# A written engine order for the last stage of a fused attention and expert kernel, and spare products beside the last four weight pieces

## The chip, the cores and the metric

The kernel runs on one core of a Trainium2 chip. Five engines work side by side, each through its own instructions in order: TensorE (PE, the matrix products; its weight loads are listed as PEld), VectorE (DVE), ScalarE (ACT), GpSimd (POOL) and SyncE (SP), whose queue issues the DMA transfers here. The metric is the device time of one execution in microseconds (us), as the median of several runs. A profile is one more execution with a recorder on.

## The reference

Three layers follow each other on 4608 tokens of width 512. Attention with pooled keys gives `x`; a soft mixture of 8 experts with 32 slots mixes it; a feed-forward layer with a softmax gate and a layer norm ends it.

```python
logits = x @ phi                                   # 4608 x 32
d = softmax(logits, over tokens); slot_input = d.T @ x
slot_out[e] = relu(slot_input[e] @ w1[e]) @ w2[e]  # 8 experts, 4 slots each
x = softmax(logits, over slots) @ slot_out

h = x @ w_in                                       # 4608 x 1024
solu = h * softmax(h)
ln = (solu - mean(solu)) / sqrt(var(solu) + 1e-6) * g_ln
out = ln @ w_out                                   # 4608 x 512
```

## The kernel before

The first half of the program computes attention, the logits and the slots. Then the expert weights stream in. The second expert layer takes `w2` in 16 pieces of 1 MB; `second(e, fh)` multiplies each piece as it lands (L856). After some pieces PE also runs a spare product, whose result nobody reads: `ident` times a part of the piece just used (L887). The dictionary `DUM` says after which pieces, and how many columns; before, after pieces 9, 10 and 11. The spare result shares its PSUM bank with `pcs`, the column sums of `w_out` that `out_sums` adds up (L848, L849). What comes after piece 15 is a chain: copies of the slot outputs (ACT L901), small products `ps` (PE L904), their copy `so` (DVE L908), the products `pM` of the slots with `w_in` (PE L924), and their copies (ACT L928), from which the first rows of `h` are computed. Part of `w_in` still has to be converted from doubles to floats beside that (ACT L745, L746; DVE L747, L748; POOL or DVE L749), and the last products `pM` wait for it.

The last stage goes over 36 tiles of 128 tokens. For tile `i` the steps are: `front_pe` (PE L1084: a pair of products makes `h`, in one of two pairs of PSUM banks), `front_max` (DVE L1089), `front_exp` (ACT L1096), `front_u` (DVE L1102, frees `h`), `front_mean` (POOL L1108), `front_square` (ACT L1113), `front_stats` (POOL, eight small instructions, L1119 to L1129; L1124 makes `sr`, L1126 makes `b`); then `turn_scale` (ACT L1138), `turn_high` (DVE L1151) and `turn_low` (DVE L1155), whose results two transposing DMAs turn (SP L1159 and L1162); then `products` (PE: 16 products with the high half `vhi`, L1174 and L1175, and 8 with the low half `vlo`, L1177, added up in one of two PSUM banks `o`); then `rows_out` (ACT L1187 copies `o` to `ob`, which frees the bank; every third tile a DMA writes the rows). The fronts run `LAG` = 4 tiles ahead of the products.

Up to a step called `E` each engine's order is written out in a list of step names, and kept. From there to the end, `mctx.close()` leaves the order to a scheduler, except for the last tile's products, which are cut in two halves of 256 columns (L1274 to L1279):

```python
    run("E")
    mctx.close()
    run("")
    for m in range(NPRO, NT):
        j = m + LAG
        if j < NT:
            front(j)
        if j - 1 < NT:
            turn(j - 1)
        if m < NT - 1 or not LS:
            products(m, 0, 8)
            rows_out(m)
```

Of the kernel before, what the change touches and what calls it, by code (L numbers as in the profile page):

```python
# [8 lines left out]
F32 = mybir.dt.float32  # L9
# [10 lines left out]
P = 128  # L20
# [3 lines left out]
NT = NP * NB * NR  # L24
# [5 lines left out]
DM = 512  # L30
DF = 1024
NE = 8
NFC = DF // P
# [15 lines left out]
LS = 2  # L49
# [36 lines left out]
def moe_attention_kernel(ctx: ExitStack, tc, q, k, v, phi, w1, w2, w_in, w_out, g, out):  # L86
# [151 lines left out]
    psE = None  # L238
    actx = ExitStack()
    if True:  # L240
# [166 lines left out]
        def turn(n, c):  # L407

            pt = st["pt", n, c] = psA.tile([P, NR, P], F32, tag="at", bufs=B.get("at",2), name=f"pt{n}{c}")
            for r in range(NR):  # L410
                pe.transpose(pt[:, r, :], a_buf[n % NA][:, r, CH[c]:CH[c] + P], ident)  # L411
# [282 lines left out]
    psE = ectx.enter_context(tc.tile_pool(name="psE", bufs=1, space=PSUM, reuse_waits="tile"))  # L694
# [31 lines left out]
    if True:  # L726
        ex = ctx.enter_context(tc.tile_pool(name="ex", bufs=1, side="left", reuse_waits="tile"))
        cvp = ctx.enter_context(tc.tile_pool(name="cvp", bufs=2, side="left", reuse_waits="tile"))
        mctx = ExitStack()
# [108 lines left out]

        p2 = psE.tile([P, DM], F32, name="p2")

        DUM = {9: (512,), 10: (512,), 11: (512,)}
        spare = psE.tile([P, DM], F32, name="spare")
        csum = T_all.rearrange("p g s -> p (g s)")

        def out_sums(c):
# [8 lines left out]
        def second(e, fh):  # L854
            for c in range(4):
                pe.matmul(p2[32 * c:32 * c + 32, :], hTm[:, 4 * fh + c, 32 * e:32 * e + 32], w2t[e, fh, c],  # L856
                          start=(e == 0 and fh == 0), stop=(e == NE - 1 and fh == 1), tile_position=(0, 32 * c))
# [8 lines left out]
        for x in range(2 * NE):  # L866
# [18 lines left out]
            second(x // 2, x % 2)  # L885
            for nn in DUM.get(x, ()):
                pe.matmul(spare[:, 0:nn], ident, w2t[x // 2, x % 2, 3][:, 0:nn], start=True, stop=True)  # L887
# [6 lines left out]
        def op(name, needs, f, *args):  # L894
            ops[name] = allops[name] = needs.split(), f, args
# [44 lines left out]
        for c in (6, 7):  # L940
# [9 lines left out]
                 'Gy6 R4 Fe9 Ga7 P5a Ff9 P5bl Gc7 Ff8 R5 Gx7 Fg8 Fg9 Ga8 Gb8 Gy7 Gx8 Gc8 Gy8 K1').split()  # L950
        assert sorted(set(steps)) == sorted(steps)
# [2 lines left out]
        def run(until):  # L954
            while steps:
                name = steps.pop(0)
                if name == until:
                    return done.add(name)
                needs, f, args = ops.pop(name)
                assert done.issuperset(needs), (name, needs)  # L960
                f(*args)
                done.add(name)
# [14 lines left out]
    LAG = 4  # L977
# [153 lines left out]
    def front(i):  # L1131
        for f in (front_pe, front_max, front_exp, front_u, front_mean, front_square, front_stats):
            f(i)
# [34 lines left out]
    def products(i, c0, c1, what="hl"):  # L1168
        hi, lo = hi_t[i], lo_t[i]
        if c0 == 0 and "h" in what:  # L1170
            po_t[i] = ps2.tile([P, DM], F32, tag="o", name=f"o{i}")
        po = po_t[i]
        for c in range(c0, c1) if "h" in what else ():
            pe.matmul(po, hi[:, c, :], W_hi[:, c, :], start=(c == 0), stop=False)  # L1174
            pe.matmul(po, hi[:, c, :], W_lo[:, c, :], start=False, stop=False)  # L1175
        for c in range(c0, c1) if "l" in what else ():
            pe.matmul(po, lo[:, c, :], W_hi[:, c, :], start=False, stop=(c == NFC - 1))  # L1177

    def rows_scaled(i):
        blk, r = divmod(i, NR)  # L1180
        if r == 0:
            o_t[blk] = wk2.tile([P, NR, DM], F32, name="ob")
        ob = o_t[blk][:, r, :]
        if i < NRAW:
            act.activation(ob, csum, AF.Copy, scale=rs_t[i][:, 0:1])
        else:
            act.activation(ob, po_t.pop(i), AF.Copy, scale=rs_t.pop(i))  # L1187

    def rows_sum(i):
        y, ob = rs_t.pop(i), o_t[i // NR][:, i % NR, :]  # L1190
        dve.scalar_tensor_tensor(ob, po_t.pop(i), y[:, 1:2], ob, ALU.mult, ALU.add)

    def rows_kept(i):
        blk, r = divmod(i, NR)
        if blk == NT // NR - 1:
            sp.dma_start(out[blk, :, DM * r:DM * r + DM], o_t[blk][:, r, :])
        elif r == NR - 1:
            sp.dma_start(out[blk], o_t.pop(blk).rearrange("p r d -> p (r d)"))

    def rows_out(i):  # L1200
        rows_scaled(i)
        if i < NRAW:
            rows_sum(i)
        rows_kept(i)
# [44 lines left out]
            op(f"R{i}", f"P{i}bl", rows_scaled, i)  # L1249
    op("K0", f"Q{NR - 1}", rows_kept, NR - 1)  # L1250
    op("K1", f"R{2 * NR - 1}", rows_kept, 2 * NR - 1)
    run("E")
    mctx.close()
    run("")
    assert not ops, ops.keys()
    for m in range(NPRO, NT):
        j = m + LAG
        if j < NT:
            front(j)
        if j - 1 < NT:  # L1260
            turn(j - 1)
        if m < NT - 1 or not LS:
            products(m, 0, 8)
            rows_out(m)

    if LS:

        hi, lo, r, ob = hi_t[NT - 1], lo_t[NT - 1], rs_t[NT - 1], o_t[NT // NR - 1][:, NR - 1, :]
        for x in range(LS):
            w = DM // LS  # L1270
            cols = slice(w * x, w * x + w)
            po = ps2.tile([P, DM], F32, tag="vT" if x % 2 else "o", name=f"o{NT - 1}{x}")[:, 0:w]
            for c in range(NFC):
                pe.matmul(po, hi[:, c, :], W_hi[:, c, cols], start=(c == 0), stop=False)  # L1274
                pe.matmul(po, hi[:, c, :], W_lo[:, c, cols], start=False, stop=False)  # L1275
            for c in range(NFC):
                pe.matmul(po, lo[:, c, :], W_hi[:, c, cols], start=False, stop=(c == NFC - 1))  # L1277
            act.activation(ob[:, cols], po, AF.Copy, scale=r)  # L1278
            sp.dma_start(out[NT // NR - 1, :, DM * (NR - 1):DM * NR][:, cols], ob[:, cols])  # L1279


# [39 lines left out]
```

## Time and profile before

| | |
|---|---|
| median of 3 runs | 449.43 us (447.93 to 451.49) |
| the profiled execution, own time | 448.71 us |
| its span in the trace | 446.9 us |
| PE busy in the span | 397.3 us (89%) |
| DVE, ACT, POOL busy | 314.6, 296.9, 236.8 us |
| matmul group L1174, idle before it | 5.1 us, of which 4.9 after ACT's `ob` |

The span is what the trace covers; the time adds 1.8 us around it. An engine's busy time adds up its instructions; for PE their ends are modelled and overlap, so that start-to-start distances say more than busy shares. Idle time in a row stands in brackets with the instruction that ended it.

### The profile page before, as it was taken

How to read it: one execution, taken by the hardware profiler on the slowest of the kernel's cores; microseconds unless marked ns; L12 is line 12 of the kernel's file. 1: busy time of each engine (PE TensorE's matmuls, PEld its weight loads, DVE VectorE, ACT ScalarE, POOL GpSimd, SP SyncE). 2: the span in 40 equal slices, each digit the busy share in tenths (PEclk: the TensorE clock that was granted, in tenths of full speed). 3: DMA queues.
4: the chain of work that ended last, by engine and by line, in shares of the span. 5: the costliest groups of instructions: out<-in, count | busy, mean ns of one | idle time of the engine just before them, and what ended most of it. 6: DMA issues, size and time to landing. Idle time of an engine off the chain costs nothing. (4 is left out here: it accounts for less than half of the span.)

```text
span 446.9 us, 8280 instructions
## 1 busy us (share of the span) xinstructions
PE 397.3 (89%) x2977; PEld 230.8 (52%) x2977; DVE 314.6 (70%) x513; ACT 296.9 (66%) x664; POOL 236.8 (53%) x427
## 2 busy tenths in 40 slices
PE   4689979987999797877979999999999999999897
PEld 4578868866977423321335544444444444444445
DVE  4897995799863634796489997667677776776730
ACT  3588976767795508763458987666667676666651
POOL 5588775568331046953105787656464464554620
PEclk9989996999899898989699999999999999999999
DMA  8999999673779798999000199565564763955853
GB/s 260 414 394 418 397 416 354 215 248 129 264 293 341 255 346 333 381 417 415 34 0 1 25 205 179 94 160 144 93 164 90 170 154 63 184 136 103 166 127 108
DMA packets 87801, 97.07 MB, mean 217 GB/s; under 512 B 70097, under 2 KB 74961, under 8 KB 82769
## 3 DMA queue, kind: packets, MB, share of 16 engines
q1 hardware_dynamic: 87760, 96.55, 68.6%
q8 instruction: 23, 0.38, 0.3%
q14 instruction: 18, 0.14, 0.1%
HBM read 70.32 MB, written 9.44 MB: 178 GB/s over the span
## 5 line engine op out<-in xcount | busy, mean ns | idle before, releaser
L1174 PE MATMUL o<-W_hi,vhi 128*128 128x512 f16 x280 | 106.2, 379 | 5.1 <-ACT ob L1187 4.9
L1175 PE MATMUL o<-W_lo,vhi 128*128 128x512 f16 x280 | 106.1, 379 | 0.0
L1177 PE MATMUL o<-W_hi,vlo 128*128 128x512 f16 x280 | 66.5, 379 | 0.0
L366 PE MATMUL sc<-BD,qT 128*128 128x144 f32 x320 | 53.3, 314 | 14.0 <-ACT BD L307 7.2
L1113 ACT ACTIVATE e<-u,nmu 128x1024 f32<-128x1024 f32 x33 | 37.9, 1149 | 26.6 <-POOL nmu L1108 26.6
L366 PEld LDWEIGHTS sc<-BD,qT 128*128 128x128 f32 x320 | 46.8, 210 | 16.9 <-POOL sel L264 6.6
L1138 ACT ACTIVATE v<-u,b,sr 128x1024 f32<-128x1024 f32 x33 | 40.8, 1237 | 21.7 <-POOL b L1126 21.7
L1102 DVE CUSTOM_DVE_ANT_0 u<-h,e 128x1024 f32<-128x1024 f32 x33 | 40.2, 1222 | 13.3 <-ACT e L1096 13.0
L1174 PEld LDWEIGHTS <-vhi 128*128 128x128 f16 x280 | 27.3, 97 | 37.6 <-issue 7.2
L1155 DVE TENSOR_TENSOR v<-v,v 128x1024 f16<-128x1024 f32 x32 | 39.1, 1223 | 10.0 <-ACT v L1138 9.8
L1175 PEld LDWEIGHTS <-vhi 128*128 128x128 f16 x280 | 27.4, 98 | 35.1 <-issue 6.1
L405 POOL TENSOR_TENSOR a<-a,rs 128x864 f32<-128x864 f32 x23 | 37.7, 1648 | 13.4 <-DVE rs L403 7.3
L1151 DVE TENSOR_SCALAR v<-u,nmu,sr 128x1024 f16<-128x1024 f32 x32 | 26.0, 813 | 26.4 <-POOL sr L1124 26.4
L1177 PEld LDWEIGHTS <-vlo 128*128 128x128 f16 x280 | 27.2, 98 | 32.3 <-issue 0.3
L1089 DVE TENSOR_REDUCE nm<-h 128x1 f32<-128x1024 f32 x33 | 40.0, 1218 | 0.4 <-PE h L1084 0.4
L1096 ACT ACTIVATE e<-h,nm 128x1024 f32<-128x1024 f32 x33 | 36.4, 1103 | 5.5 <-DVE nm L1089 5.5
L411 PE MATMUL pt<-ident,a 128*128 128x128 f32 x180 | 31.6, 293 | 4.5 <-ACT aT L417 3.0
L377 DVE TENSOR_REDUCE nmax<-sc 128x6 f32<-128x432 f32 x48 | 28.1, 597 | 7.3 <-PE sc L366 7.2
L417 ACT ACTIVATE aT<-pt 128x384 f32<-128x384 f32 x60 | 28.0, 491 | 6.9 <-PE pt L411 6.4
L1124 POOL TENSOR_TENSOR sr<-z,exponents 128x3 f32<-128x3 f32 x33 | 29.0, 879 | 2.6
L411 PEld LDWEIGHTS pt<-ident,a 128*128 128x128 f32 x180 | 21.3, 147 | 9.4 <-ACT aT L417 3.1
L389 ACT ACTIVATE a<-dd 128x432 f32<-128x432 f32 x36 | 19.8, 567 | 9.2 <-DVE ssum L396 4.7
(237 smaller groups left out, 772.0 us busy)
## 6 DMA issues: line engine op xcount, KB each, us to landing
w<-in_w_dram SPq DMA_DIRECT2D x16, 1024.0 KB, 10.5
vT<-in_v_dram SPq DMA_DIRECT2D x8, 1152.0 KB, 14.4
out_dram<-ob SPq DMA_DIRECT2D x11, 768.0 KB, 3.9
w<-in_w_dram SPq DMA_DIRECT2D x16, 512.0 KB, 5.5
kT<-in_k_dram SPq DMA_DIRECT2D x7, 1152.0 KB, 13.8
qT<-in_q_dram SPq DMA_DIRECT2D x7, 768.0 KB, 14.5
qT<-in_q_dram SPq DMA_DIRECT2D x8, 384.0 KB, 16.4
raw<-in_w_in_dram SPq DMA_DIRECT2D x3, 1024.0 KB, 9.5
```

The lines of the kernel that those rows point to most:

```text
L366: pe.matmul(sc[:, r].rearrange("p h j -> p (h j)"), qT[n][:, hp, x, :], BD[b % NBD][:, hp, :], start=(i == 0), stop=(i == len(hv) - 1))
L405: eng.tensor_tensor(av, av, rs.unsqueeze(3).to_broadcast([P, NR, 4, J]), ALU.mult)
L411: pe.transpose(pt[:, r, :], a_buf[n % NA][:, r, CH[c]:CH[c] + P], ident)
L1089: dve.tensor_reduce(nm, ft[i][0], axis=AX.X, op=ALU.max, negate=True)
L1096: act.activation(e, hv, AF.Exp, bias=nm, accum_out=st[:, 0:1])
L1102: dve.tensor_tensor_reduce(u, hv, e, 1.0, 0.0, ALU.mult, ALU.add, st[:, 1:2])
L1113: act.activation(e, u, AF.Square, bias=nmu, accum_out=st[:, 2:3])
L1138: act.activation(v, u, AF.Identity, bias=b, scale=sr[:, 0:1])
L1155: dve.tensor_tensor(v2, u_t[i]["v"], u_t[i]["v1"], ALU.subtract)
L1174: pe.matmul(po, hi[:, c, :], W_hi[:, c, :], start=(c == 0), stop=False)
L1175: pe.matmul(po, hi[:, c, :], W_lo[:, c, :], start=False, stop=False)
L1177: pe.matmul(po, lo[:, c, :], W_hi[:, c, :], start=False, stop=(c == NFC - 1))
```

## The change

There are two parts. First, the written order no longer ends at `E`: `mctx.close()` moves to the very end, so that all engines keep the order in which the code is written, and the loop over tiles is written in pieces. Within one round PE does the high products of tile `m`, then the front pair of tile `m + 4`, then the low products of `m`; ACT does the exponential of `m + 4`, the rows of `m`, the scaling of `m + 3`, the square of `m + 4`; DVE the maximum of `m + 4`, the high half of `m + 3`, `u` of `m + 4`, the low half of `m + 3`. Second, `DUM` gets entries for pieces 12 to 15, and the spare result gets a PSUM bank of its own.

```diff
-        DUM = {9: (512,), 10: (512,), 11: (512,)}
-        spare = psE.tile([P, DM], F32, name="spare")
+        DUM = {9: (512,), 10: (512,), 11: (512,), 12: (512,), 13: (512,), 14: (512,), 15: (256,)}
+        spare = psE.tile([P, DM], F32, name="spare", tag="warm")
...
-    run("E")
-    mctx.close()
     run("")
     assert not ops, ops.keys()
     for m in range(NPRO, NT):
-        j = m + LAG
-        if j < NT:
-            front(j)
-        if j - 1 < NT:
-            turn(j - 1)
-        if m < NT - 1 or not LS:
-            products(m, 0, 8)
+        f, t = m + LAG, m + LAG - 1
+        front_there, turn_there = f < NT, t < NT
+        if m < NT - 1:
+            products(m, 0, NFC, "h")
+        if front_there:
+            front_pe(f)
+        if m < NT - 1:
+            products(m, 0, NFC, "l")
+        if front_there:
+            front_max(f)
+            front_exp(f)
+        if m < NT - 1:
             rows_out(m)
+        if turn_there:
+            turn_high(t)
+            turn_high_out(t)
+            turn_scale(t)
+        if front_there:
+            front_u(f)
+            front_mean(f)
+            front_square(f)
+        if turn_there:
+            turn_low(t)
+            turn_low_out(t)
+        if front_there:
+            front_stats(f)
...
             sp.dma_start(out[NT // NR - 1, :, DM * (NR - 1):DM * NR][:, cols], ob[:, cols])
+    mctx.close()
```

What moves on ACT in the middle of the last stage, first before. `e,st<-h` is the exponential, `ob<-o` the rows, `v<-u` the scaling, `e,st<-u` the square; the number behind `o` or `h` names the tile's bank.

```order
L1096 ACTIVATE e,st<-h_3972,nm 128x1024
L1138 ACTIVATE v<-u,b,sr 128x1024
L1113 ACTIVATE e,st<-u,nmu 128x1024
L1187 ACTIVATE ob<-o_4007,r 128x512
L1138 ACTIVATE v<-u,b,sr 128x1024
L1096 ACTIVATE e,st<-h_4034,nm 128x1024
L1187 ACTIVATE ob<-o_4069,r 128x512
L1113 ACTIVATE e,st<-u,nmu 128x1024
L1096 ACTIVATE e,st<-h_4095,nm 128x1024
L1138 ACTIVATE v<-u,b,sr 128x1024
L1113 ACTIVATE e,st<-u,nmu 128x1024
L1187 ACTIVATE ob<-o_4130,r 128x512
```

The twelve rows serve three tiles, each in another order. The same place after the change:

```order
L1096 ACTIVATE e,st<-h_3992,nm 128x1024
L1187 ACTIVATE ob<-o_3975,r 128x512
L1138 ACTIVATE v<-u,b,sr 128x1024
L1113 ACTIVATE e,st<-u,nmu 128x1024
L1096 ACTIVATE e,st<-h_4054,nm 128x1024
L1187 ACTIVATE ob<-o_4037,r 128x512
L1138 ACTIVATE v<-u,b,sr 128x1024
L1113 ACTIVATE e,st<-u,nmu 128x1024
```

Each tile now has the same four in the same order, with the rows right behind the exponential. On PE, around one front pair, before:

```order
L1177 LDWEIGHTS vlo
L1177 MATMUL o_3390<-W_hi,vlo 128x512
L1084 MATMUL h_3417<-MS,cS 128x512 x2
L1174 LDWEIGHTS vhi
L1174 MATMUL o_3452<-W_hi,vhi 128x512
```

The pair stood between two tiles' products. After the change:

```order
L1175 LDWEIGHTS vhi
L1175 MATMUL o_3420<-W_lo,vhi 128x512
L1084 MATMUL h_3437<-MS,cS 128x512 x2
L1177 LDWEIGHTS vlo
L1177 MATMUL o_3420<-W_hi,vlo 128x512
```

It stands inside one tile's products, between the high and the low ones. On PE at the last four weight pieces (`w_60` to `w_74`), as a piece of the difference:

```order
 L856 MATMUL p_2401<-w_60_2335,hTm 32x512 x4
+L887 MATMUL spare<-w_60_2335,ident 128x512
 L856 MATMUL p_2401<-w_64_2337,hTm 32x512 x4
+L887 MATMUL spare<-w_64_2337,ident 128x512
 L856 MATMUL p_2401<-w_70_2339,hTm 32x512 x4
+L887 MATMUL spare<-w_70_2339,ident 128x512
 L856 MATMUL p_2401<-w_74_2341,hTm 32x512 x4
-L904 MATMUL ps<-sel_73,s_2630 128x32 x4
+L887 MATMUL spare<-w_74_2341,ident 128x256
+L904 MATMUL ps<-sel_73,s_2634 128x32 x4
```

Each piece is followed by a spare product, and the last one stands ahead of the small products `ps`. Since the spare result no longer holds their bank, the column sums `pcs` of the first seven chunks, which stood together behind the spare product of piece 11, now stand spread among pieces 9 to 11.

## Rows read from the trace of the kernel before

**Rows 1.** Waits of one instruction on another, 310 to 440 us: total, times, longest.
```profile
PE o L1174 <- ACT ob L1187: 4.9, 13, 0.9
```
**Rows 2.** PE in order of time: start, duration, engine, line, operation, tiles.
```profile
256.77 1.29 PE L1084 MATMUL h<-MS,cS 128*128 128x512 f32 x4
...
302.32 0.82 PE L1084 MATMUL h<-MS,cS 128*128 128x512 f32 x2
307.98 0.82 PE L1084 MATMUL h<-MS,cS 128*128 128x512 f32 x2
...
415.37 0.82 PE L1084 MATMUL h<-MS,cS 128*128 128x512 f32 x2
```
**Rows 3.** The chain that ended last: start, duration, what.
```profile
433.20 0.22 PE o L1174
...
438.38 0.11 PE o L1274
```
**Rows 4.** All engines in order of time, 359 to 367 us.
```profile
359.55 1.24 ACT L1138 ACTIVATE v<-u,b,sr 128x1024 f32<-128x1024 f32 x1 [1.10 <-POOL b L1126]
...
360.46 0.22 POOL L1108 TENSOR_SCALAR nmu<-st 128x1 f32<-128x1 f32 x1
...
360.71 1.15 ACT L1113 ACTIVATE e<-u,nmu 128x1024 f32<-128x1024 f32 x1
360.82 1.23 DVE L1155 TENSOR_TENSOR v<-v,v 128x1024 f16<-128x1024 f32 x1 [0.38 <-ACT v L1138]
...
361.86 0.67 ACT L1187 ACTIVATE ob<-o,r 128x512 f32<-128x512 f32 x1
361.96 1.22 DVE L1089 TENSOR_REDUCE nm<-h 128x1 f32<-128x1024 f32 x1
...
362.58 0.38 PE L1174 MATMUL o<-W_hi,vhi 128*128 128x512 f16 x1 [0.26 <-ACT ob L1187]
...
363.21 1.12 ACT L1096 ACTIVATE e<-h,nm 128x1024 f32<-128x1024 f32 x1 [0.68 <-DVE nm L1089]
...
363.59 0.81 DVE L1151 TENSOR_SCALAR v<-u,nmu,sr 128x1024 f16<-128x1024 f32 x1 [0.41 <-POOL sr L1124]
...
364.45 1.23 DVE L1102 CUSTOM_DVE_ANT_0 u<-h,e 128x1024 f32<-128x1024 f32 x1
...
365.60 1.22 DVE L1155 TENSOR_TENSOR v<-v,v 128x1024 f16<-128x1024 f32 x1
...
365.78 1.12 POOL L1108 TENSOR_SCALAR nmu<-st 128x1 f32<-128x1 f32 x1 [0.61 <-DVE st L1102]
...
366.94 1.15 ACT L1113 ACTIVATE e<-u,nmu 128x1024 f32<-128x1024 f32 x1 [1.39 <-POOL nmu L1108]
```
**Rows 5.** The DMA queue in order of time, 250 to 270 us.
```profile
263.20 2.66 SPq L1162 DMA_TRANSPOSE vlo<-v  x2
```
**Rows 6.** DMA issues on the page: queue, kind, count, median us from issue to landing.
```profile
vlo<-v SPq DMA_TRANSPOSE x32, 3.1
```
**Rows 7.** Stretches: length, busy (instructions) of each engine, granted TensorE clock, DMA.
```profile
206.00:213.00 7.00, 4.13 (x35) 0.63 (x32) 1.95 (x3) 0.00 (x0) 2.38 (x1) 1.00 0.98 401
214.00:220.00 6.00, 6.00 (x24) 2.43 (x24) 4.00 (x6) 2.85 (x6) 1.35 (x1) 0.50 0.01 4
```
**Rows 8.** All engines in order of time, around the last weight pieces.
```profile
202.06 1.12 PE L887 MATMUL spare<-w,ident 128*128 128x512 f32 x2
...
206.37 1.95 PE L856 MATMUL p<-w,hTm 128*32 128x512 f32 x16
...
212.25 1.06 PE L856 MATMUL p<-w,hTm 128*32 128x512 f32 x8 [1.44 <-DMA w<-in_w_dram]
...
213.82 1.90 PE L904 MATMUL ps<-sel,s 128*128 128x32 f32 x8 [0.50 <-ACT s L901]
...
220.02 0.13 PEld L924 LDWEIGHTS pM<-win,so 128*32 128x32 f32 x1 [1.20 <-DVE win L749]
...
221.58 0.60 ACT L928 ACTIVATE hTm<-pM 128x512 f32<-128x512 f32 x1 [0.40 <-PE pM L924]
```

2 rows, old and new, of the table steps are left out of this document.

## The prediction

> **What bounds the kernel now.** I read the waits first, to see which engine the last stage waits for. PE, the busiest engine, waited 13 times for ACT's `ob` before a tile's first product, 4.9 us in all [rows 1]. Then I read PE in order of time, for the distance from one front pair to the next. Early in the stage it is 5.66 us (302.32 to 307.98); nothing but products fills it, since a tile's 24 products take 5.18 us (433.20 to 438.38) and the pair the other 0.48. From 307.98 to 415.37 there are 18 tiles, which at 5.66 would take 101.88 us; they took 107.39 [rows 2, 3]. So PE lost 5.51 us there. From the front pair at 415.37 to the last tile's halves at 438.38 are 23.01 us; the pair and four tiles need 0.48 + 4 x 5.18 = 21.20, so 1.81 more were lost. Together 7.3 us is the most that a better order of the last stage can give; below that PE is the bound, whatever the others do.
>
> Why does ACT come late? One round of the trace shows it: `ob` runs at 361.86 without idle time ahead of it, that is, its turn on ACT came late, and the product at 362.58 starts as it ends [rows 4]. The bank it frees belongs to the tile before the last one, whose products had ended a whole tile earlier. So it is the place of `ob` in ACT's queue that costs, and not the work: ACT and DVE each have idle time in the same rows.
>
> Last I read the stretch after the expert weights. The granted clock is 1.00 of full (2.4 GHz) from 206 to 213 us and 0.50 (1.2 GHz) from 214 to 220, after PE had been busy only 4.13 of 7 us [rows 7]. Nothing is being loaded then, and the chain of PE, ACT and DVE steps sets the end.
>
> **The written order, loop by loop.** With the order fixed, each engine repeats its round, and the round can't be shorter than any closed loop of waits. I sum the loops from start-to-start distances [rows 4].
>
> PE: 5.66, as above.
>
> Loop A, through the rows: maximum to exponential 1.25 (361.96 to 363.21), exponential 1.12, `ob` 0.67, scaling to low half 1.27 (359.55 to 360.82), low half to the next maximum 1.14 (360.82 to 361.96): 5.45.
>
> Loop B, through the statistics: square to high half 2.88 (360.71 to 363.59), high half 0.81, `u` to mean 1.33 (364.45 to 365.78), mean to square 0.25 (360.46 to 360.71): 5.27.
>
> Both are below 5.66, so PE sets the pace, and the others wait for its front pair. At that pace I place one round, counted from the start of the maximum: exponential 1.25, `u` 1.25 + 1.24 = 2.49 (363.21 to 364.45), `ob` 2.37, scaling 3.04, low half 4.31; mean 2.49 + 1.33 = 3.82, ended at 4.04; square when the scaling is done, 4.28; the high half of this tile 4.28 + 2.88 = 7.16, which is 1.50 after the next maximum and ends at 2.31, in time for `u` at 2.49. `ob` of tile `m` ends 3.04 after the maximum, which starts 0.85 after the front pair (its 0.82 [rows 2] and a wake-up); its bank is wanted by tile `m + 2`, 0.48 + 1.73 + 5.66 = 7.87 after that pair. So PE no longer waits for `ob`, with 4 us to spare: the 7.3 us come back.
>
> Moved DMAs: each transposing DMA follows its half in SP's queue, and the row DMA of every third tile stands ahead of the high half's transpose and waits for `ob`. That delays the transpose to 3.04 after the maximum instead of 1.50 + 0.81, less than 1 us; the products want it three rounds later, so it costs nothing.
>
> The entry into the loop costs something. Before, PE had the high products of tiles 4 and 5 ahead of the low ones of both, which gave the transposes time. Now each tile's low products follow its own high ones. From the front pair at 256.77 [rows 2] PE reaches the low products of tile 5 after two pairs, two high parts of 3.45 and one low part of 1.73: 9.59, at 266.36. Their transpose started at 263.20 [rows 5], and such a transpose lands 3.1 us after issue [rows 6], 266.3: just in time. In the written order it stands behind the high transpose of tile 6, whose high half now comes after one low half (1.23) and two maxima (1.22 each) on DVE. Bounds: 0 and 2.5, taken as 0.8, since the maxima were ahead of it before too. The last stage gives 7.3 - 0.8 = 6.5; bounds 4.8 and 7.3.
>
> **The spare products.** Pieces 12 and 13 take 0.97 us each (206.37, 1.95 for two); a spare product of 512 columns took 1.12 to the end of its row [rows 8], and 256 columns would take about half. PE starts piece 12 at 206.37; three pieces with spares, 3 x (0.97 + 1.12) = 6.27, end at 212.64 against 212.25, when the last piece is there. If the passes overlap as in the pieces it is early; so the last piece comes 0 to 0.9 late, taken as 0.4. The spare after piece 15 stands ahead of the small products, but they wait for ACT's copies anyway (212.25 + 1.06 to 213.82).
>
> In return PE is busy nearly throughout from 206 to 214, and I expect full clock up to the products `pM`. At double clock the small products, 1.90, would take 0.95, if they scale; the last `pM`, 220.02 to the copy at 221.58, 1.56, would take about 0.95. What lies between (the word conversion on DVE and POOL) doesn't scale, but begins behind the copy of the small products, so it moves up with them. Gain 0.95 + 0.6 - 0.4 = 1.1; bounds: 1.5, and a loss of 0.9 if the clock falls all the same and the delay is at its largest. The column sums that move up among pieces 9 to 11 run while weights are loading, and the loads were all issued by then: nothing.
>
> **Rivals.** (1) GpSimd's mean falls under VectorE's low half, and loop B sets the pace. The mean takes 0.22 alone and 1.12 when a low half starts 0.18 ahead of it (365.60, 365.78), and the square then starts 1.16 after the mean instead of 0.25 [rows 4]. Loop B becomes 6.18, longer than PE's 5.66, and feeds itself: the late square makes the statistics, the high half and `u` late, and behind a late `u` the low half starts at once, ahead of the mean. It decides once the high half is about 0.45 later than placed above (0.18 until `u` slips, 0.27 until its mean meets the low half). Price: the trace's 18 tiles ran at 5.97; 26 tiles at 0.21 more are 5.5, less the 1.1 of the clock: 448.71 + 4.4 = 453.1, slower. Against it: at 5.66 the round has room, and any wait for PE restores the order.
>
> The Trainium skill ("SBUF — State Buffer", Who interferes with whom) says that a VectorE instruction with two SBUF inputs contends with a GpSimd one that reads SBUF, and that issue order decides who blocks. By that rule the mean, first at 3.82, would win and hold the low half back by up to 0.22, which puts loop A at 5.67, level with PE: the sum stays. The trace agrees on the late case (1.12); no row here shows the early one.
>
> (2) Two banks `o` are too few, and the wait stays in another place. Then only the clock gives: 447.6. Against it: the late `ob` at 361.86 was not waiting for PE. The Trainium skill ("Perfetto Trace Analysis", Optimization Strategy) says that the same gap repeating on the engine that should be saturated can mean too little PSUM for the next tile; by it the gap would survive the new order. The rows say that the bank was full but done with, so the order can cure it.
>
> (3) The spare products don't hold the clock: the change doesn't do there what it says. 448.71 - 6.5 + 0.4 = 442.6.
>
> (4) The entry stalls more, or small delays hold the loops at about 5.8 a tile, 0.14 x 26 = 3.6 back: 444 to 446.
>
> **How the numbers follow.** The forecast is 448.71 - 6.5 - 1.1 = 441.1 for the profiled execution, which was 0.72 below the median of 449.43; so 441.8 as a median. Shifted likewise, the rivals give 453.8, 448.3, 443.3 and 445 to 447. Chances: forecast 0.55, (1) 0.08, (2) 0.08, (3) 0.15, (4) 0.14. The forecast's own bounds are 440.6 (7.3 + 1.5) and 443.5; noise of the runs lowers the lower end to 440.0. With (3) and (4) the upper end is 447.0; what is left out is (1), (2) and a little more, 0.17. About 1% is what a measurement of this kernel can tell from no change: below 444.9 is faster, above 453.9 slower. Faster: the forecast, (3) and a quarter of (4), 0.74. Slower: the worse half of (1) and what I haven't thought of, 0.05. The rest, 0.21, is the same.
>
> **What would show it.** Right: front pairs 5.66 apart from tile 12 to the end, no idle time before L1174 put down to `ob`, each `ob` right behind an exponential, means of 0.22; granted clock 1.00 from 206 to beyond 217, `ps` near 1 us. Wrong: means of 1.12 in every round and pairs 6.1 or more apart (1); L1174 still behind `ob` (2); 0.50 after the last piece (3); idle time on PE before the low products of tiles 4 to 6 (4). What I trust least are the eight POOL instructions of the statistics, which the high and low halves can both hold up.

## The result, and the profile after

The changed kernel took 443.23 us in the median of 8 runs (440.87 to 446.11), the kernel before 449.98 in the median of 8 (446.65 to 454.14). The ratio is 0.9875, with an interval of 0.983 to 0.992: faster by 1.25%. The profiled execution took 445.94 us, with a span of 444.2. The ratios leave out runs that took over 1.5% longer than the fastest of their kernel; for the entry in pairs, further down, these are three of six, and nothing rests on that ratio.

PE of the kernel after in order of time; the pairs of the fronts alone, early and late in the stage:

```profile
275.67 0.82 PE L1084 MATMUL h<-MS,cS 128*128 128x512 f32 x2
...
309.65 0.82 PE L1084 MATMUL h<-MS,cS 128*128 128x512 f32 x2
315.32 0.82 PE L1084 MATMUL h<-MS,cS 128*128 128x512 f32 x2
...
417.32 0.82 PE L1084 MATMUL h<-MS,cS 128*128 128x512 f32 x2
```

From 275.67 to 417.32 are 25 tiles in 141.65 us, 5.67 each; every distance between is 5.66 or 5.67. Before, 18 tiles had lost 5.51 us against that pace [rows 2].

The waits of the kernel after, 310 to 440 us, in the same columns as before [rows 1]:

```profile
ACT e L1096 <- DVE nm L1089: 32.1, 20, 1.6
...
PEld L1177 <- issue: 5.6, 20, 0.3
```

No row of PE's L1174 behind ACT's `ob` is left; what PE still shows is time in its own issue. The others wait now, ACT for the maximum 1.6 us a tile, and that costs nothing.

All engines but PE in the kernel after, one round; the idle time ahead stands in brackets, with its releaser:

```profile
344.51 1.23 DVE L1089 TENSOR_REDUCE nm<-h 128x1 f32<-128x1024 f32 x1 [0.24 <-PE h L1084]
...
345.77 1.11 ACT L1096 ACTIVATE e<-h,nm 128x1024 f32<-128x1024 f32 x1 [1.61 <-DVE nm L1089]
345.98 0.81 DVE L1151 TENSOR_SCALAR v<-u,nmu,sr 128x1024 f16<-128x1024 f32 x1 [0.24 <-POOL sr L1124]
...
346.88 0.68 ACT L1187 ACTIVATE ob<-o,r 128x512 f32<-128x512 f32 x1
347.01 1.22 DVE L1102 CUSTOM_DVE_ANT_0 u<-h,e 128x1024 f32<-128x1024 f32 x1 [0.22 <-ACT e L1096]
347.44 1.24 ACT L1138 ACTIVATE v<-u,b,sr 128x1024 f32<-128x1024 f32 x1
...
348.33 0.23 POOL L1108 TENSOR_SCALAR nmu<-st 128x1 f32<-128x1 f32 x1 [1.32 <-DVE st L1102]
348.59 1.15 ACT L1113 ACTIVATE e<-u,nmu 128x1024 f32<-128x1024 f32 x1
...
348.71 1.23 DVE L1155 TENSOR_TENSOR v<-v,v 128x1024 f16<-128x1024 f32 x1 [0.47 <-ACT v L1138]
348.92 1.07 POOL L1120 TENSOR_TENSOR y<-y 128x1 f32<-128x1 f32 x1
```

Counted from the maximum at 344.51: exponential 1.26, high half 1.47, `ob` 2.37, `u` 2.50, scaling 2.93, mean 3.82 of 0.23 us, square 4.08, low half 4.20. The round placed ahead had 1.25, 1.50, 2.37, 2.49, 3.04, 3.82, 4.28 and 4.31. Against [rows 4], `ob` now stands right behind the exponential in every round of the loop that has one.

The chain that ended last, after:

```profile
412.47 1.74 PE o L1177 x8
418.14 1.74 PE o L1177 x8
423.34 1.73 PE o L1177 x8
428.52 1.73 PE o L1177 x8
```

5.67 with a front pair, then 5.18 without one, as at the end of before [rows 3].

What is left on the page of idle time ahead of L1174, after:

```profile
L1174 PE MATMUL o<-W_hi,vhi 128*128 128x512 f16 x280 | 107.1, 382 | 1.4 <-DMA vhi<-v 1.4
```

It was 5.1 us. The 1.4 is one stop, at the entry. PE there, after:

```profile
263.21 0.81 PE L1084 MATMUL h<-MS,cS 128*128 128x512 f32 x2
263.87 1.90 PE L1177 MATMUL o<-W_hi,vlo 128*128 128x512 f16 x8
267.18 0.39 PE L1174 MATMUL o<-W_hi,vhi 128*128 128x512 f16 x1 [1.41 <-DMA vhi<-v]
```

And SP's DMA queue at the same place, after:

```profile
260.69 1.23 SPq L1162 DMA_TRANSPOSE vlo<-v  x1
261.97 0.57 SPq L1198 DMA_DIRECT2D out_dram<-ob  x1
262.70 4.67 SPq L1159 DMA_TRANSPOSE vhi<-v  x2
```

PE stops for the high half of tile 5, whose transpose begins at 262.70, behind tile 4's low transpose and a row DMA. Before, the transpose of tile 5 that mattered was the low one, at 263.20 [rows 5]. The distance from the pair at 263.21 to the next at 275.67 is 12.46; two low parts (3.46), two high parts (6.90) and a pair (0.48) need 10.84. So the entry costs 1.62.

Stretches after the weight pieces, after, in the columns of [rows 7], with one more stretch:

```profile
206.00:213.00 7.00, 7.00 (x38) 1.68 (x36) 3.56 (x5) 0.55 (x1) 2.40 (x1) 1.00 1.01 417
214.00:220.00 6.00, 5.98 (x38) 2.14 (x34) 2.21 (x5) 3.41 (x7) 0.79 (x1) 1.00 0.13 48
...
229.00:233.00 4.00, 3.59 (x11) 1.80 (x12) 2.26 (x4) 0.95 (x2) 0.32 (x2) 0.57 0.00 0
```

PE is busy for 7.00 of 7 us and keeps 2.4 GHz to 220, but falls to 1.2 GHz for most of 229 to 233. And PE around the last two pieces, after:

```profile
212.98 1.07 PE L856 MATMUL p<-w,hTm 128*32 128x512 f32 x8
213.98 1.13 PE L887 MATMUL spare<-w,ident 128*128 128x512 f32 x2
215.03 1.06 PE L856 MATMUL p<-w,hTm 128*32 128x512 f32 x8
216.03 0.70 PE L887 MATMUL spare<-w,ident 128*128 128x256 f32 x2
216.60 1.08 PE L904 MATMUL ps<-sel,s 128*128 128x32 f32 x8
```

The pieces are 2.05 apart, 6.15 us from piece 12 (208.88) to the last one. Before, it was 5.88 (206.37 to 212.25), and half of that was waiting for pieces 14 and 15 to land (1.43 and 1.44, of which [rows 8] show the last). Now PE no longer waits for the last one; it is PE that makes it late. The small products take 1.08 instead of 1.90.

Two marks divide the profiles for what follows. The pair of tile 8 (256.77 before [rows 2], 259.28 after) to the end of the span is the last stage: 190.13 before, 184.92 after, 5.21 less. The issue of the last raw load of `w_in` (SP L194, 202.28 before, 203.90 after; two halves, of which the first is meant) to the first front pair, that of tile 3 (PE L1084, 236.56, 239.10), is the stretch of the spare products: 34.28 before, 35.20 after, 0.92 more. The issue itself came 1.62 later after; that is scatter, since over the 14 profiles here it came anywhere from 198.42 to 204.49, and in two profiles of the changed kernel itself at 203.90 and 200.47 (e8).

### The profile page after: what moved, and what is told of

Same layout as the page of the kernel before. It is cut to its first block, busy times and chain, and to the rows that moved or that the text cites. A ratio compares the mean times of both kernels' runs of the same rounds, so it can differ in the third digit from the quotient of the medians.

```text
span 444.2 us, 8295 instructions
## 1 busy us (share of the span) xinstructions
PE 400.7 (90%) x2985; PEld 231.6 (52%) x2985; DVE 319.6 (72%) x513; ACT 294.8 (66%) x664; POOL 250.7 (56%) x427
## 4 chain that ended last, share of the span: by engine, by line
PE 65%; DVE 11%; ACT 10%; DMA 6%; issue 4%; POOL 2%; SPq 1%; ACTq 0%; DVEq 0%; POOLq 0%
PE o L1174 13%; PE o L1175 13%; PE o L1177 13%; PE sc L366 5%; PE h L1084 3%; PE p L700 3%; PE plt L427 2%; ACT a L383 2%; DMA W_hi<-in_w_out_dram 2%; PE pt L411 2%; ACT aT L417 2%; PE p L856 2%; DMA kT<-in_k_dram 2%; PE spare L887 2%; PE pG L496 1%
## 5 line engine op out<-in xcount | busy, mean ns | idle before, releaser
L1174 PE MATMUL o<-W_hi,vhi 128*128 128x512 f16 x280 | 107.1, 382 | 1.4 <-DMA vhi<-v 1.4
L1174 PEld LDWEIGHTS <-vhi 128*128 128x128 f16 x280 | 27.6, 99 | 35.4 <-DMA vhi<-v 1.9
L1177 PEld LDWEIGHTS <-vlo 128*128 128x128 f16 x280 | 25.0, 98 | 33.6 <-issue 7.7
L1120 POOL TENSOR_TENSOR y<-y 128x1 f32<-128x1 f32 x33 | 30.4, 922 | 2.7
L1108 POOL TENSOR_SCALAR nmu<-st 128x1 f32<-128x1 f32 x33 | 8.3, 253 | 37.5 <-DVE st L1102 37.4
```

## The experiments

**The order alone** (e1: the changed kernel with the spare products of before).

```diff
-        DUM = {9: (512,), 10: (512,), 11: (512,), 12: (512,), 13: (512,), 14: (512,), 15: (256,)}
-        spare = psE.tile([P, DM], F32, name="spare", tag="warm")
+        DUM = {9: (512,), 10: (512,), 11: (512,)}
+        spare = psE.tile([P, DM], F32, name="spare")
```

> The written order alone; the spare products and their bank are as before. Theory A (the order carries the whole gain; the spares as made bring the last weight piece late by about 1.1 us and leave a later fall of the clock, so they cost 0 to 1): ratio to before 0.984 to 0.988, as fast as the full change or up to 1 us faster; front pairs 5.67 apart; clock 0.50 for some 6 us after the last weight piece. Theory B (as I predicted: order 6.5, spares 1.1): 1 to 1.5 us slower than the full change, ratio about 0.990.

443.15 us (6 runs), ratio 0.9887 (0.9835 to 0.994). The last stage took 185.16, so the order alone brings what the whole change brought there. The stretch of the spare products took 32.66, less than in either profile of the kernel before, though nothing in it is changed.

**The spare products alone** (e2: the kernel before with the other `DUM` and the tag).

```diff
-        DUM = {9: (512,), 10: (512,), 11: (512,)}
-        spare = psE.tile([P, DM], F32, name="spare")
+        DUM = {9: (512,), 10: (512,), 11: (512,), 12: (512,), 13: (512,), 14: (512,), 15: (256,)}
+        spare = psE.tile([P, DM], F32, name="spare", tag="warm")
```

> The spare products after pieces 12 to 15 and their own bank alone; the last stage is ordered by the scheduler as before. Theory A: ratio 1.000 to 1.003; the last piece starts about 1.1 us after it has landed, the small products take about 1.1 instead of 1.9, and the clock falls to 0.50 somewhere in the 12 us behind. Theory B: ratio 0.997 to 0.998.

448.67 us (12 runs), ratio 1.0032 (0.9994 to 1.007): nothing gained. The last stage took 190.38, as before.

**One spare product, after piece 14** (e3), and the same kernel once more (e11).

```diff
-        DUM = {9: (512,), 10: (512,), 11: (512,), 12: (512,), 13: (512,), 14: (512,), 15: (256,)}
+        DUM = {9: (512,), 10: (512,), 11: (512,), 14: (512,)}
```

> The full change, but of the four new spare products only the one after piece 14 is kept. Both theories of the spares' cost say that the last piece then starts when it lands (0 to 0.2 late instead of 1.1). If the clock holds after that, this is about 1 us faster than the full change; if a spare less lets the clock fall at the last piece, the small products take 1.9 again and it is as fast as the order alone.

> The kernel with the one spare product behind piece 14 once more, for a second look at its clock. If its granted clock of 1.00 throughout is its own, the stretch from the last raw load's issue to the first front pair is 32.4 to 32.9 us again; if the fall of the clock comes and goes by chance, as it did between two runs of the changed kernel, it can be 33.5 to 34.5.

442.08 us (12 runs), ratio 0.987 (0.9828 to 0.9912), which can't be told from the 0.9875 of the whole change; the single run of e11 took 440.47. From the raw load to the first front pair 32.65 and 32.33 us, small products 1.08 in both. Stretches of e3, columns as above:

```profile
214.00:220.00 6.00, 5.04 (x26) 1.54 (x26) 4.00 (x6) 3.44 (x7) 1.35 (x1) 1.00 0.01 3
222.00:234.00 12.00, 8.97 (x37) 3.95 (x36) 9.73 (x26) 6.19 (x14) 0.46 (x2) 1.00 0.00 0
```

The clock held, with less PE work than the changed kernel had. And PE waits for the last piece again:

```profile
212.29 1.06 PE L856 MATMUL p<-w,hTm 128*32 128x512 f32 x8 [0.40 <-DMA w<-in_w_dram]
```

**Narrow spare products** (e10).

```diff
-        DUM = {9: (512,), 10: (512,), 11: (512,), 12: (512,), 13: (512,), 14: (512,), 15: (256,)}
+        DUM = {9: (512,), 10: (512,), 11: (512,), 12: (128,), 13: (128,), 14: (512,)}
```

> The changed kernel with spare products of 128 columns instead of 512 behind pieces 12 and 13, 512 behind 14, none behind 15. Theory: the four spare products cost in two ways, by making the last piece 1.1 us late and by a fall of the clock after the small products. Here only the first goes: the last piece begins less than 0.3 us after it has landed. From the last raw load's issue to the first front pair it is then 32.4 to 32.9 us if the clock holds at 1.00, and about 34.1 if it falls to 0.50 for some 3.4 us after the small products as in most runs of the changed kernel (35.2). Rival: the lateness is not from the width of the spare products but from their count, and the last piece is still 0.6 us late or more: 33.2 or more with the clock at 1.00. Ratio to before 0.985 to 0.990 in either case.

443.85 us (7 runs), ratio 0.9879 (0.983 to 0.9929). PE of e10 at pieces 12 to 14:

```profile
209.23 0.49 PE L887 MATMUL spare<-w,ident 128*128 128x128 f32 x2
209.65 1.06 PE L856 MATMUL p<-w,hTm 128*32 128x512 f32 x8
...
211.06 1.06 PE L856 MATMUL p<-w,hTm 128*32 128x512 f32 x8
```

Pieces 12 to 14 are 1.41 apart instead of 2.05, the last one begins 9.54 after the raw load instead of 11.13, and it is 32.55 to the first front pair with the clock at 1.00. With the same count of spares ahead of the last piece, narrow ones take 1.27 less from piece 12 to it (4.88 instead of 6.15); the other 0.32 is that piece 12 itself began earlier.

**The changed kernel and the kernel before, unchanged, again** (e8, e12).

> The changed kernel itself once more, to see whether the fall of the clock some 12 us after the last piece is there each time. Theory A (it follows from the spares keeping the clock up to the products pM and then PE being half idle for some us): clock 0.50 for about 3.4 us between 227 and 234 us, first front pair of tile 3 35.2 us after the last load is issued. Theory B (chance): clock 1.00 throughout and 33.5.

> The kernel before, unchanged, for a second look at its clock after the weight pieces. If the fall to 0.50 for 6.8 us is its own, the stretch from the last raw load's issue to the first front pair is 34.0 to 34.5 us again; if it comes and goes by chance, 32.6 to 33.5.

e8: 442.05 us (6 runs), ratio 0.9898 (0.985 to 0.9946). e12: 444.56 us (one run). The same stretch of e8, and then a stretch of e12:

```profile
222.00:234.00 12.00, 8.96 (x41) 4.22 (x40) 9.79 (x27) 6.46 (x15) 0.92 (x5) 1.00 0.00 0
```
```profile
224.00:227.00 3.00, 3.00 (x9) 1.11 (x8) 1.89 (x3) 0.04 (x1) 0.00 (x0) 0.52 0.00 0
```

In this profile of the changed kernel the clock did not fall between the last piece and the first front pair, and in this one of the kernel before it fell some 10 us later than in [rows 7], and for half as long; the small products took 1.08 there without any added spare. So one profile of either is not the kernel. All 14, the two middle columns in us after the issue of the last raw load, the last one, between the last piece and the first front pair, in us of the span:

| kernel | last piece begins | first front pair | clock at 1.2 GHz |
|---|---|---|---|
| before | 9.97 | 34.28 | 213.9 to 220.7 |
| before again (e12) | 9.01 | 33.08 | within 223 to 227 |
| order alone (e1) | 9.32 | 32.66 | within 214 to 218 |
| all spares: after | 11.13 | 35.20 | within 229 to 233 |
| all spares: e2, e4, e5 | 11.15, 11.12, 11.16 | 35.22, 35.18, 35.23 | 3 to 4 us within 227 to 234 |
| all spares: e6 | 10.62 | 34.69 | within 223 to 228 |
| all spares: e8 | 10.62 | 33.63 | never |
| after 14 alone: e3, e7, e9, e11 | 9.64, 9.43, 8.73, 9.31 | 32.65, 32.44, 31.74, 32.33 | never |
| narrow (e10) | 9.54 | 32.55 | never |

**The scaling ahead of the rows** (e5): one block of the loop moved.

```diff
-        if m < NT - 1:
-            rows_out(m)
         if turn_there:
             turn_high(t)
             turn_high_out(t)
             turn_scale(t)
+        if m < NT - 1:
+            rows_out(m)
```

> The full change with one swap in the written round: ACT scales the tile for the turn ahead of copying the rows. Theory (the prediction's first rival as a mechanism): the low half then starts about 3.65 after the maximum, straight behind u, and before the mean, due at 3.82; the mean takes 1.12 instead of 0.22, the square, the statistics, the high half and u become late in turn, and once PE's lead is used up the front pairs stand 6.1 to 6.2 apart instead of 5.67: 8 to 10 us slower than the full change, ratio to before 1.00 to 1.015. Rival (the mean has slack, or the instruction that starts first doesn't hold POOL up): means of 0.22, pairs 5.67 apart, as fast as the full change.

453.02 us (4 runs), ratio 1.0143 (1.0086 to 1.02). The pairs stay 5.66 apart to tile 19, then they are 6.07 to 6.10 apart; the means are 6.09 to 6.11 apart, and take 1.12 to 1.14, from 278.24 on, that is from the start of the loop. All engines of e5 late in the stage, and its wait of L1174 from 310 to 440 us:

```profile
381.70 1.22 DVE L1155 TENSOR_TENSOR v<-v,v 128x1024 f16<-128x1024 f32 x1
381.88 1.13 POOL L1108 TENSOR_SCALAR nmu<-st 128x1 f32<-128x1 f32 x1 [1.02 <-DVE st L1102]
...
383.04 1.15 ACT L1113 ACTIVATE e<-u,nmu 128x1024 f32<-128x1024 f32 x1 [1.12 <-POOL nmu L1108]
```
```profile
PE o L1174 <- ACT ob L1187: 6.1, 19, 0.8
```

That is the first rival as it was described: the low half starts 0.18 ahead of the mean, which takes 1.13 instead of 0.23, the square begins 1.16 behind it, and the loop through the statistics sets the pace.

**The rows one round late** (e6).

```diff
-        if m < NT - 1:
-            rows_out(m)
+        if m > NPRO:
+            rows_out(m - 1)
```

> The full change, but each round copies the rows of the tile before instead of its own; work and banks are the same. Theory (it is the place of the copy in ACT's queue that made PE wait, not the number of banks as such): PE waits about 1.7 us for ob ahead of each tile's first product, since the loop front pair, maximum, exponential, copy, high products closes in 0.85 + 1.25 + 1.12 + 0.72 + 3.45 = 7.4 us; pairs 7.3 to 7.4 apart, 42 to 45 us slower than the full change. Rival (the copy's place doesn't matter, the banks alone do): 5.67 apart.

479.14 us (one run); pairs 7.21 apart, a little less than the 7.3 to 7.4 expected. Its wait of L1174:

```profile
PE o L1174 <- ACT ob L1187: 25.0, 18, 1.4
```

With the same banks and the same work, this wait is 0, 4.9 or 25.0 us. Between 0 and 25.0 only the place of `ob` differs, and with it the time for which a bank stays full; between 4.9 and 0 the whole order does.

**The entry** in three steps: the high half of tile 5 and its transpose ahead of tile 4's low half (e4); the same further ahead, with one spare product (e7); the same, and PE's high products of tiles 4 and 5 ahead of the low ones of both (e9). Of the written list (`Gb5`, `Gx5` are tile 5's high half and transpose, `Fg5` its statistics, `Fe6` tile 6's mean, `P4a` and `P5a` the high products, `P4bl` and `P5bl` the low ones, `R3` tile 3's rows; e9 also moves `Gy5`, tile 5's low transpose, ahead of tile 6's high one, which the excerpt leaves out):

```diff
-P3bl Fa8 Fe6 Gx4 P4a Ff6 Gc4 Fa9 Fg5 Gy4 K0 Fe7 Gb5 Ga5 ... Gx5 ... R3 Ff7 P4bl ... R4 Fe9 Ga7 P5a Ff9 P5bl
+P3bl Fa8 Fe6 Gx4 P4a Ff6 Fa9 Fg5 Gb5 Gx5 Gc4 Gy4 K0 Fe7 Ga5 ... R3 Ff7 P4bl ... R4 Fe9 Ga7 P5a Ff9 P5bl
+P3bl Fa8 Gx4 Fg5 Fe6 Gb5 Gx5 P4a Ff6 Gc4 Fa9 Gy4 K0 Fe7 Ga5 ... R3 Ff7 P4bl ... R4 Fe9 Ga7 P5a Ff9 P5bl
+P3bl Fa8 Gx4 Fg5 Fe6 Gb5 Gx5 P4a Ff6 Gc4 Fa9 Gy4 K0 Fe7 Ga5 R3 Fb8 P5a ... Ff7 P4bl ... R4 Fe9 Ga7 Ff9 P5bl
```

> The full change, with the high half of tile 5 and its transpose moved ahead of the low half of tile 4 and its transpose in the written list. Theory: PE's one stop at the entry (1.6 us ahead of tile 5's high products, put down to the transpose) goes, because that transpose starts some 2 us earlier; 1.0 to 1.6 us faster than the full change. Rival: the stop is the price of having one tile's low products right behind its high ones and comes back as a wait for tile 4's or tile 5's low transpose; no change.

> The full change with only the spare product after piece 14 of the four new ones, and with tile 5's statistics ahead of tile 6's mean on POOL, its high half and transpose ahead of tile 4's low ones. Theory (the entry stop comes from the statistics being late, which hold the high half): the high transpose of tile 5 starts within 2 us of the front pair of tile 8 instead of 3.4; PE's stop ahead of tile 5's products, 1.4 us, goes, and the run is 1 to 1.5 us faster than the one with the spare after piece 14 alone. Rival (one tile's low products right behind its high ones need both transposes early, and the queue can only bring one): the stop moves to the low products of tile 4 or 5 and nothing is gained.

> The one spare product behind piece 14, and at the entry the high products of tiles 4 and 5 both ahead of the low ones of both, with the high half of tile 5 and its transpose early. Theory: the entry stops because the transposes are wanted too soon after their halves, whichever half it is; with 3.45 us of high products and a front pair between them the low transposes of tiles 4 and 5 have landed when PE wants them. Then PE's idle time between the front pairs of tiles 9 and 10 is 0.1 to 0.6 us instead of 1.6, the way from the front pair of tile 8 to the end 183.5 to 184.5 us instead of 184.9, the median 1 to 1.5 us below that of the kernel with one spare product alone (442.08), ratio to before 0.984 to 0.986. Rival: the halves themselves come too late on VectorE, and PE then waits for the low transposes of tile 4 or 5 as it did when only the high half of tile 5 was moved up: idle time of 1.5 to 2.6 us, the way to the end 184.9 to 185.5, ratio 0.987 to 0.990.

e4: 445.29 us (12 runs), ratio 0.9917 (0.9868 to 0.9967); the entry took 12.56 instead of 12.46, the last stage 184.67. e7: 443.01 (6 runs), ratio 0.9892 (0.9838 to 0.9946); entry 13.42, last stage 185.48. The stop has only moved, to the low products, as PE of e7 shows:

```profile
262.53 1.90 PE L1177 MATMUL o<-W_hi,vlo 128*128 128x512 f16 x8 [0.65 <-DMA vlo<-v]
...
269.48 1.90 PE L1177 MATMUL o<-W_hi,vlo 128*128 128x512 f16 x8 [1.59 <-DMA vlo<-v]
```

e9: 443.12 us in the median of all 6 runs (436.88 to 445.11) against 448.44, that is 0.988 by the medians; the ratio, 0.9797 (0.9738 to 0.9856), rests on three runs. PE of e9:

```profile
256.11 0.81 PE L1084 MATMUL h<-MS,cS 128*128 128x512 f32 x2
...
257.38 0.38 PE L1174 MATMUL o<-W_hi,vhi 128*128 128x512 f16 x1 [0.46 <-ACT ob L1187]
...
260.83 3.62 PE L1177 MATMUL o<-W_hi,vlo 128*128 128x512 f16 x16
...
267.55 0.81 PE L1084 MATMUL h<-MS,cS 128*128 128x512 f32 x2
```

Entry 11.44, 1.02 less than in the changed kernel; the low products of both tiles run as one row of 16 with no stop, and what is left is a stop of 0.46 for `ob` ahead of tile 5's high products. The last stage took 183.83, the shortest of all, and the profiled span was 436.0. By the trace this is the best version, 1.1 us better in the last stage than the changed kernel; by the medians it can't be told from e3, where 1 to 1.5 us less had been expected.

## Why the prediction was right, and where not

**The bound and the round: right.** The place of `ob` in ACT's queue was the cause. PE's pace of 5.66 held from the entry to the end, and the placed round came true within 0.11 us, but for the square, 0.20 early. e6 shows the cause from the other side, and e1 that it needs no help from the spares. The second rival (two banks are too few) falls with that. The Trainium skill ("Perfetto Trace Analysis", Optimization Strategy) says that a repeating gap can mean too little PSUM; that is not what made this one, since the banks are the same and it is gone.

**The first rival: a real mechanism that this order avoids.** It was said to decide from about 0.45 us of delay of the high half. In the changed kernel the high half is 1.47 behind the maximum and the mean ends 0.15 before the low half begins. In e5 the scaling stands ahead of `ob`, and the loop tips at once; PE's pairs, which run ahead, show it only from tile 19 on. The pace of 6.10 is near the 6.18 that the rival was priced at. e5 tips it by an early low half and not by a late high half, so the 0.45 itself is not tested. The Trainium skill ("SBUF — State Buffer", Who interferes with whom), by which issue order decides who blocks, agrees with what the trace shows: POOL's L1120, begun 0.19 to 0.21 after the low half, took 1.07 to 1.09 in every round of the loop, against 0.20 beside the maximum (e5, 383.36). In the written order that falls on an instruction with time to spare.

**The entry: right in kind, mis-sized.** It was taken as 0.8 of bounds 0 to 2.5, and cost 1.62; and PE stopped at the high transpose of tile 5, not at its low one. The step that failed looked only at the low transposes. The high half of tile 5 now stands behind tile 4's low half, and its transpose behind a row DMA. In e4 and e7 an earlier high half on DVE only moved the stop to the low transposes. e9 gives PE the order of before again, which the prediction named as what the change gave up, and gets 1.02 back; since it also moves tile 5's low transpose up, which of the two does it is not shown.

The 7.3 us was itself 0.17 too high: it counts from the pair at 415.37 in order of time to the halves at 438.38 in the chain, but in order of time they begin at 438.21:

```profile
438.21 0.27 PE L1274 MATMUL o<-W_hi,vhi 128*128 128x256 f16 x1
```

And the entry had lost 0.29 before, too: 11.61 from the pair at 256.77 to the next at 268.38, where two pairs, two high and two low parts need 11.32. So 7.44 us were lost before. After, 1.62 are lost at the entry, 0.15 in the pace, 0.19 between the last pair and the last tile's halves, and the end is 0.25 longer (the last copy to the end of the span took 3.25 before, 3.50 after). That leaves 5.2, as measured. The forecast said 6.5, with 4.8 to 7.3 as bounds.

**The spare products: the term that failed.** It was a gain of 1.1, and the profile shows a loss of 0.92, just at the far bound. The parts that the prediction priced came out nearly as said, against the profile of before: the three spares ahead of the last piece cost 0.27 (6.15 instead of 5.88 from piece 12; 0.4 was taken, out of 0 to 0.9); the small products take 0.82 less (0.95); from `so` to the copy of the last `pM` it is 5.34 instead of 5.82, 0.48 less (0.6). What failed are two terms that were put at nothing.

The first is the column sums that move up. Since the spare result has a bank of its own, the first of them stands ahead of piece 9 and waits there for `W_hi`, so piece 9 begins 7.02 us ahead of the raw load's issue instead of 9.55, and piece 12 begins 4.98 behind it instead of 4.09, 0.89 later. Piece 9 before, and then after, with piece 12:

```profile
192.73 1.06 PE L856 MATMUL p<-w,hTm 128*32 128x512 f32 x8
```
```profile
196.37 0.59 PE L848 MATMUL pcs<-W_hi,ones_h 128*128 128x512 f16 x1 [1.93 <-ACT W_hi L776]
196.88 1.94 PE L856 MATMUL p<-w,hTm 128*32 128x512 f32 x8
...
208.88 1.07 PE L856 MATMUL p<-w,hTm 128*32 128x512 f32 x8
```

In the three profiles with the shared bank (before, e12, e1) piece 12 begins 2.87 to 4.09 behind the issue, in the eleven others 4.46 to 5.02. Alone, that need not cost anything: in e3 piece 12 begins at 5.01, and PE still waits for the last piece. With wide spares behind pieces 12 to 14 there is no such wait left to take it up, and the last piece begins 1.16 later.

The second is the clock behind `pM`. It held up to `pM`, as forecast, but the forecast ended there. From the copy of the last `pM` (221.58 before [rows 8]) to the first front pair it is 16.04 instead of 14.98, 1.06 more:

```profile
223.06 0.60 ACT L928 ACTIVATE hTm<-pM 128x512 f32<-128x512 f32 x1 [0.78 <-PE pM L924]
```

In five of the six profiles with four wide spares the clock fell some 14.5 us after the last piece began, within that stretch. In e8, where it did not, the stretch took 14.98 and piece 12 began at 4.47; the sum there was a gain of 0.65. The third rival, no hold at all, was wrong in place and right in effect.

Part of the gain was not there to take, either: e12 shows the kernel before with small products of 1.08 and 33.08 to the first front pair, and e1, with the same spares, 32.66. Against these two and the profile of before the four spares as made cost 0.4 to 2.6 us, and in e8 between 0.65 less and 0.97 more; one spare after piece 14 is 0.0 to 2.5 us better in four profiles, so that a gain by it is not shown. Why the clock fell in five of six profiles with four wide spares, in all three with none added, and in none of five with one or with narrow ones, isn't settled; no run here varies it apart from the lateness.

**The sum.** By the two marks the trace gives -5.2 + 0.9 = -4.3 for the profiled execution, where the forecast was -7.6. Its own time was only 2.77 lower, because the first half came 1.62 later, which is within its scatter. The median fell by 6.75, inside the interval (3.6 to 7.7 us) and 1.4 above the forecast of 441.8. That it came so near owes something to the scatter of the first half; the traces would have put it at 445.7. Faster, as forecast, and by the order alone.

## What to carry to other kernels

When the bound engine waits for a copy out of a full bank, look first whether the copying engine came to it late or had it ready late; idle time of 0 ahead of the copy says that it stood behind other work, so its place in the queue is the first thing to change; here neither more banks nor faster work was needed. Before writing an order for a steady loop, sum each closed loop of waits, place one round, and then work through the entry tile by tile, for every DMA that is wanted there. Work that is added to hold a clock is to be priced with all that it moves, here the column sums that a new bank let forward, and up to the next mark that the clock can slow, and its effect is to be read in several profiles.

## What was not expected of the hardware

The granted clock falls at different places in executions of one kernel: at 213.9 to 220.7 and then at about 223 to 227 us in two profiles of the kernel before, at 229 to 233, or not at all between the last piece and the first front pair, in two of the changed one. The first half of the program reached the last raw load's issue anywhere between 198.42 (e6) and 204.49 us (e7); e6 and e4 (204.46) run the same instructions up to there. That scatter is as large as the effect measured; marks inside the trace were needed to see 1 us.
